# A fixed order on all engines for the first block of a fused attention and mixture-of-experts kernel, with two chunks multiplied undivided in place of eight

## The chip, the cores and the metric

The kernel runs on one core of a Trainium2 chip. A core has a matrix engine (TensorE, PE in the rows), VectorE (DVE), ScalarE (ACT) and GpSimd (POOL), each with a list of instructions of its own, and SyncE (SP), from whose queue this kernel's loads are issued. Engines wait for each other through semaphores. PEld is TensorE's loading of weights, which runs beside its products. The metric is the device time of one execution in microseconds (us).

## The reference

Attention of 2 batches, 8 heads, 768 queries and a head size of 64; its output feeds a dense two-layer network, and that one a routed network of 8 experts. Shortened:

```python
# attention: each query sees its own neighbours and one key and value per block of 32
k_sum = k.reshape(B, H, 24, 32, D).max(axis=3)
v_sum = v.reshape(B, H, 24, 32, D).mean(axis=3)
scores_l = where(abs(i - j) < 16, q @ k.T / 8, -1e9)
scores_s = q @ k_sum.T / 8 + log(32)
a = softmax(concat(scores_l, scores_s));  x = a @ concat(v, v_sum)     # 1536 x 512
# dense network, 512 -> 2048 -> 512
h = x @ w_in;  g = where(h > 0, h, exp(min(h, 0)) - 1);  x = g @ w_out
# routed network: for each token the expert e of the largest logit
e = argmax(x @ w_gate)
out = prob[e] * sigmoid(x @ w_output_gate)[e] * (relu(x @ w1[e]) @ w2[e])
```

## The kernel before

The 1536 tokens are 24 units of 64 queries, in four blocks j of 8, 4, 6 and 6 units (512, 256, 384, 384 tokens). The hidden layer of the dense network has 16 chunks c of 128. TensorE runs through all (j, c), with the attention of the next block between them: `mm_h(j,c)` forms h = x·w_in of a chunk, and two chunks later `mm_y(j,c)` adds g·w_out into one accumulator per 128 tokens.

Products keep float32 accuracy by division: an operand is split into a rounded high half and a low half, and a product is three, high·high, high·low and low·high. mm_h is 4×3 of these, mm_y one group of three per 128 tokens. "Undivided" means that mm_y multiplies the float32 operands themselves, one instruction per 128 tokens, which the trace shows as two records; the constant `C3` says for how many chunks of block 0.

What the other engines do for a chunk: ScalarE takes tanh and exp of h (`elu_act`, tiles elt and ele), VectorE forms elt and then elp, which is g (`elu_dve`). The second of these frees h's bank; there are two banks, so mm_h(j,c+2) waits for elp(j,c). For a divided chunk follow `split_g` (ScalarE gh, VectorE gl) and `split_w` (ScalarE the high half of wsp, VectorE the low one).

The weights come as 64-bit floats and are converted during block 0: per chunk and part (w_in "ri", w_out "ro") ScalarE's `conv_r` (two passes, or one for w_in chunks in `BITS`), VectorE's `conv_t` (one bit operation, or two for those in BITS) and `conv_f` (on POOL for the parts in `CP`), and for w_in the high and low halves, `conv_h` (ScalarE) and `conv_l` (VectorE). Raw w_out tiles and the wsp tiles share one pool of four buffers, the tiles of conversion, block keys ("kst") and value means ("vn1") one of five.

Orders: `START` is a list of steps by which all engines are ordered by hand, from the first maxima of keys to about the sixth chunk; `ORDER` is the order of the first loads. Behind START only TensorE's order is fixed (the loop over steps in the last function), and a scheduler places the other engines' and the queue's instructions. `PAIRS` gives the half step of a chunk at which a pair of units begins its attention, `SUM0` that of the block keys and value means of the second batch element.

Of the kernel before, what the change touches and what calls it, by code (L numbers as in the profile page):

```python
# [9 lines left out]
F32 = mybir.dt.float32  # L10
F32R = mybir.dt.float32r
# [72 lines left out]
class Prog:  # L84
# [86 lines left out]
    def conv_a(self, c, part):  # L171
        self.conv_r(c, part)
        self.conv_t(c, part)
        self.conv_f(c, part)

    def conv_b(self, c, part):
        if part == 0:
            self.conv_h(c)
            self.conv_l(c)

    def split_w(self, j, c):
        if j == 0 and c < C3:
            return
        nc = self.nc
        f = self.w[c, 1].bitcast(F32)
        w = self.ws.tile([128, 2, 512], F32R, tag="ws", name="wsp")
        nc.scalar.copy(w[:, 0], f)  # L187
        nc.vector.tensor_tensor(w[:, 1], f, w[:, 0].bitcast(F32), op=ALU.subtract)  # L188
        self.wsp[j, c] = w
# [273 lines left out]
    def x_lo(self, u):  # L463
        self.at5(u, 1)
# [19 lines left out]
    def elu(self, j, c):  # L484
        for i in range(2):
            self.elu_act(j, c, i)
        for i in range(2):
            self.elu_dve(j, c, i)

    def elu_act(self, j, c, i):  # L490
# [5 lines left out]
    def elu_dve(self, j, c, i):  # L496
# [112 lines left out]
    def part1(self):  # L609
# [10 lines left out]
        self.kT, self.cv, self.te, self.nmean = {}, {}, {}, 0  # L620
# [5 lines left out]
        pieces = [(c, p) for c in range(NF) for p in range(2)]  # L626
        wq, cq, dq = list(pieces), list(pieces), list(pieces)

        def wload(n):
            for x in wq[:n]:  # L630
                self.load_w(*x)
            del wq[:n]

        def conv(n=1):
            for _ in range(n):
                if dq and len(dq) > len(cq):
                    self.conv_b(*dq.pop(0))
                if cq and cq[0] in self.raw:
                    self.conv_a(*cq.pop(0))
# [19 lines left out]
        for j in range(1, NBLK):  # L659
            for n in range(UNITS[j]):  # L660
# [15 lines left out]
        at(14, self.route_consts)  # L676
        rank = {"at4": 0, "at3": 1, "at2": 2, "at1": 3, "at1bs": 4, "at5": 0}
        for p in range(NP):
            for hf in range(2):
                at(SUM0 + p - 2, self.load_sum, p, hf)  # L680
                at(SUM0 + p, self.red_sum, p, hf)
        for i in range(8):
            hs = SUM0 + 4 + 2 * i // 3
            at(hs - 2, self.load_v1, i)
            at(hs, self.mean_v1, i)
        at(SUM0 + 9, self.vsums2)
# [33 lines left out]
        with self.tc.manual_schedule(engines={mybir.EngineType.PE}):  # L720
            for i in range(len(steps)):
# [4 lines left out]
                wload(3)  # L726
                first = j == 0 and c in self.whole
                if j or c not in self.known:
                    self.mm_h(j, c, TB // 2 if j == 0 and c in self.half else 0)
                if not first:  # L730
                    conv()
# [6 lines left out]
                if i >= 2:
                    jj, cc = steps[i - 2]
                    if jj or cc not in self.summed:  # L740
                        self.mm_y(jj, cc)
                    if cc == NF - 1:
                        self.out_y(jj)
                if not first:
                    conv()
# [3 lines left out]
    def start_up(self):  # L749

        unit = dict(k=self.k_sum, s=self.scores, m=self.maxes, b=self.less_max, e=self.at1b, z=self.sums, r=self.recip, n=self.norm,
                    t=self.turn, c=self.turned, o=self.weighted, h=self.x_hi, l=self.x_lo, p=self.v_pad, x=self.max_k0, a=self.add_eps, M=self.mean_v0, K=self.keep_warm)
        part = dict(A=self.conv_r, B=self.conv_t, C=self.conv_f)
        self.split, self.half, self.whole, self.summed, self.known = (set() for _ in range(5))
        with self.tc.manual_schedule():
            for op in START.split():
                if op[0] == "H":
                    self.mm_h(0, int(op[1:]), 0, TB // 2)
                    self.half.add(int(op[1:]))
                    continue  # L760
                if op[0] in "GUVY":
                    c = int(op[1])
                    if op[0] == "G":
                        self.mm_h(0, c, TB // 2 if c in self.half else 0)
                        self.known.add(c)
                    elif op[0] == "Y":
                        self.mm_y(0, c)
                        self.summed.add(c)
                    else:
                        (self.elu_act if op[0] == "U" else self.elu_dve)(0, c, int(op[2]) - 1)  # L770
                        self.whole.add(c)
                    continue
                k, n = op[0], [int(i) for i in op[1:]]
                if k in unit:
                    unit[k](*n)
                elif k in part:
                    part[k](*n)
                    if k == "C" and n[1] == 1:
                        self.split.add((n[0], 1))
                elif k == "w":  # L780
                    self.window(*n)
                elif k == "P":
                    self.pad_v0()
                elif k == "D":
                    self.conv_h(*n)
                elif k == "E":
                    self.conv_l(*n)
                    self.split.add((n[0], 0))
# [811 lines left out]
```

## Time and profile before

| | |
|---|---|
| median of 3 runs | 533.13 us (532.93 to 533.65) |
| the profiled execution | 532.56 us, span 530.8 us |
| mean granted TensorE clock | 0.991 of full speed |
| TensorE busy | 515.1 us, 97% |
| VectorE busy | 332.1 us, 63% |
| ScalarE busy | 298.1 us, 56% |
| POOL busy | 55.9 us, 11% |

The times of the rows count from the start of the span. A row of a timeline gives start, duration, engine, line of the kernel, operation, output and inputs, and in brackets how long the engine was idle before and what ended that. Rows of equal instructions that follow each other are one row with a count, whose duration runs from the first start to the last end. Durations overlap a little: an instruction's last part runs beside the next one's first. [...] A wait for several semaphores is put down to the one that came last.

### The profile page before, as it was taken

What the parts mean: (1) busy time and instruction counts of PE and PEld (TensorE: products, weight loads), DVE (VectorE), ACT (ScalarE), POOL (GpSimd) and SP (SyncE); (2) the same over time, 40 slices, a digit from 0 to 9 for tenths busy, and PEclk for the clock granted to TensorE, in tenths of its full rate; (3) what the DMA queues carried; (4) which work ended last, traced back from release to release, by engine and by line L of the source; (5) the groups of instructions that cost most, each with busy time, mean ns of one, the idle gap of its engine ahead of it and who ended that gap; (6) DMA issues with size and microseconds to landing.
All of it is one profiled execution on the core that took longest, in us unless ns stands there. A gap on an engine that the chain in (4) does not pass through costs nothing. (4 is left out here: it accounts for less than half of the span.)

```text
span 530.8 us, 9764 instructions
## 1 busy us (share of the span) xinstructions
PE 515.1 (97%) x3299; PEld 404.9 (76%) x3299; DVE 332.1 (63%) x932; ACT 298.1 (56%) x704; POOL 55.9 (11%) x102
## 2 busy tenths in 40 slices
PE   8998999969999999999999999999999999999995
PEld 6485666758898888888999888888888566576884
DVE  4878999985687977785656799759421001545510
ACT  4798998834486767565546547443242232656521
POOL 2522000000000000000000000212511110100001
PEclk9999999979999999999999999999999999999999
DMA  8999834421022212100001006310498799494601
GB/s 288 404 404 314 278 123 143 147 71 31 27 103 81 75 36 91 57 25 16 0 2 61 1 25 233 101 61 1 122 354 279 299 340 348 157 364 137 220 23 43
DMA packets 37131, 78.08 MB, mean 147 GB/s; under 512 B 3951, under 2 KB 9807, under 8 KB 37072
## 3 DMA queue, kind: packets, MB, share of 16 engines
q1 hardware_dynamic: 34752, 70.02, 38.6%
q0 software_dynamic: 2320, 7.34, 3.9%
q8 instruction: 28, 0.46, 0.4%
q14 instruction: 31, 0.25, 0.2%
HBM read 100.37 MB, written 6.55 MB: 201 GB/s over the span
## 5 line engine op out<-in xcount | busy, mean ns | idle before, releaser
L481 PE MATMUL h<-xh,wi 128*128 128x384 f32 (+2 forms) x528 | 145.8, 344 | 6.5 <-DVE elp L506 6.5
L481 PEld LDWEIGHTS h<-xh,wi 128*128 128x128 f32 x528 | 95.0, 191 | 16.1 <-DVE elp L506 6.4
L536 PE MATMUL y<-wsp,gh 128*128 128x512 f32 x320 | 101.3, 398 | 0.0
L481 PE MATMUL h<-xl,wi 128*128 128x384 f32 (+2 forms) x264 | 88.2, 334 | 0.0
L536 PEld LDWEIGHTS y<-wsp,gh 128*128 128x128 f32 x320 | 57.7, 188 | 10.2 <-ACT ele L494 0.3
L536 PE MATMUL y<-wsp,gl 128*128 128x512 f32 x160 | 62.9, 393 | 0.0
L1255 DVE TENSOR_TENSOR holdl<-S,holdh 128x512 fp32r<-128x512 f32 x22 | 15.2, 690 | 72.5 <-ACT holdh L1251 53.7
L1223 PE MATMUL h<-w2s,holdh 128*128 128x512 f32 x176 | 59.9, 401 | 0.0
L1266 PE MATMUL y<-w2s,holdh 128*128 128x512 f32 x176 | 59.1, 398 | 0.0
L500 DVE SCALAR_TENSOR_TENSOR elt<-ele,elt 128x384 f32<-128x384 f32 (+2 forms) x64 | 36.4, 568 | 32.1 <-ACT ele L494 31.8
L481 PEld LDWEIGHTS h<-xl,wi 128*128 128x128 f32 x264 | 50.4, 191 | 5.0 <-issue 1.7
L494 ACT ACTIVATE elt<-h 128x384 f32<-128x384 f32 (+2 forms) x64 | 31.0, 484 | 32.5 <-PE h L481 31.6
L187 ACT CAST wsp<-wo 128x512 fp32r<-128x512 f32 x56 | 34.4, 617 | 21.7 <-PE y L536 21.7
L516 ACT CAST gh<-elp 128x384 fp32r<-128x384 f32 (+2 forms) x56 | 27.8, 496 | 31.0 <-DVE elp L506 21.7
L188 DVE TENSOR_TENSOR wsp<-wo,wsp 128x512 fp32r<-128x512 f32 x56 | 38.6, 689 | 8.7 <-ACT wsp L187 8.2
L1266 PEld LDWEIGHTS y<-w2s,holdh 128*128 128x128 f32 x176 | 33.1, 188 | 8.5 <-issue 1.6
L1223 PEld LDWEIGHTS h<-w2s,holdh 128*128 128x128 f32 x176 | 33.1, 188 | 8.1 <-ACT w2s L1291 0.8
L363 ACT ACTIVATE e<-e,nb 128x120 f32<-128x120 f32 x88 | 33.6, 384 | 10.0 <-DVE nb L350 10.0
L517 DVE TENSOR_TENSOR gl<-elp,gh 128x384 fp32r<-128x384 f32 (+2 forms) x56 | 30.0, 535 | 12.8 <-ACT gh L516 12.4
L1297 DVE TENSOR_TENSOR w2s<-wo,w2s 128x512 fp32r<-128x512 f32 x48 | 30.8, 686 | 8.8 <-ACT w2s L1291 7.3
L506 DVE SCALAR_TENSOR_TENSOR elp<-elt,h 128x384 f32<-128x384 f32 (+2 forms) x64 | 35.2, 550 | 1.2
L536 PEld LDWEIGHTS y<-wsp,gl 128*128 128x128 f32 x160 | 30.0, 188 | 6.9 <-DVE gl L517 0.3
(291 smaller groups left out, 845.8 us busy)
## 6 DMA issues: line engine op xcount, KB each, us to landing
wo<-in_w SPq DMA_DIRECT2D x9, 2048.0 KB
wo<-in_w SPq DMA_DIRECT2D x18, 1024.0 KB
ri<-in_w_in SPq DMA_DIRECT2D x16, 512.0 KB
ro<-in_w_out SPq DMA_DIRECT2D x16, 512.0 KB
wo<-in_w SPq DMA_DIRECT2D x32, 256.0 KB
w2p<-in_w SPq DMA_DIRECT2D x32, 256.0 KB
w2q<-in_w SPq DMA_DIRECT2D x24, 256.0 KB
k<-in_kw SPq DMA_DIRECT2D x18, 192.0 KB
```

The source lines that it names most:

```text
L187: nc.scalar.copy(w[:, 0], f)
L188: nc.vector.tensor_tensor(w[:, 1], f, w[:, 0].bitcast(F32), op=ALU.subtract)
L363: nc.scalar.activation(e[:, p], e[:, p], AF.Exp, bias=nb[:, p:p + 1], scale=-1.0, accum_out=sm[:, p:p + 1])
L481: nc.tensor.matmul(h, lhsT=w[:, wl, k * 128:k * 128 + 128], rhs=x[:, k, a:b], start=(n == 0), stop=(n == 11))
L494: self.nc.scalar.activation(self.te[j, c][i], self.h[j, c], AF.Exp if i else AF.Tanh, scale=1.0 if i else 0.5)
L500: nc.vector.scalar_tensor_tensor(t, e, 1.0, t, op0=ALU.add, op1=ALU.mult)
L506: nc.vector.scalar_tensor_tensor(p, t, 0.0, h, op0=ALU.min, op1=ALU.max)
L517: nc.vector.tensor_tensor(gl, p, gh.bitcast(F32), op=ALU.subtract)
L536: nc.tensor.matmul(self.y[j][t], lhsT=gx[:, sl], rhs=wx, start=(c == 0 and n == 0), stop=(c == NF - 1 and n == len(ops) - 1))
L1223: nc.tensor.matmul(self.h[s, hf], lhsT=x[:, k], rhs=w, start=(n == 0), stop=(n == 11))
L1266: nc.tensor.matmul(self.y2[s], lhsT=g[:, ks], rhs=w, start=(i == 0 and n == 0), stop=(i == 7 and n == 2))
L1297: (self.nc.gpsimd if eng == "Pool" else self.nc.vector).tensor_tensor(e[1], self.rw[i], e[0].bitcast(F32), op=ALU.subtract)
```

## The change

C3 falls from 8 to 2, so that mm_y of chunks 2 to 7 of block 0 is divided too, with split_w and split_g for them. BITS loses the w_in chunks 5, 10, 12 and 14. START is now the order of the whole of block 0 on all engines and of SyncE's loads (steps that begin with L), with the attention of units 8 to 11, the block keys and value means of the second batch element and the splits in single steps; ORDER and SUM0 are gone, and the loop begins at block 1. CP, WE, KE, NE, RADD and PADA, which say on which engine a conversion or a small step of a unit runs, have other entries. From mm_h(1,2) on TensorE's instructions are in the same order in both kernels.

```diff
-C3 = 8
+C3 = 2
-BITS = (0, 1, 2, 3, 5, 6, 8, 10, 12, 14)
-PAIRS = {8: 9, 10: 20, 12: 35, 14: 45, 16: 54, 18: 65, 20: 74, 22: 83}
+BITS = (0, 1, 2, 3, 6, 8)
+PAIRS = {12: 35, 14: 45, 16: 54, 18: 65, 20: 74, 22: 83}
-SUM0 = 26
-ORDER = "k3 k0 k2 k1 Q0 c0 Q1 c1 V4 V1 V2 W7 w1 V3 V0 Q2 W6 w1 w1 w1 w1 w1 w1 w1 w1 w1 w1 w1"
-NE = "PVVPPVPV"
-CP = ((1, 0), (1, 1))
-START = ...
+NE = "VVVPVVPV"
+CP = ((0, 0),)
+START = ...
     def split_w(self, j, c):
-        if j == 0 and c < C3:
-            return
...
+        self.w_high(j, c)
+        self.w_low(j, c)
...
-        for x in ORDER.split():
...
-        at(14, self.route_consts)
+        at(2 * NF, self.route_consts)
...
-            for i in range(len(steps)):
+            for i in range(NF, len(steps)):
...
     def start_up(self):
...
+        load = dict(k=self.load_k0, Q=self.load_q0, V=self.load_v0, W=self.load_kw, c=self.load_c, w=self.load_w, q=self.load_q, v=self.load_v, s=self.load_sum, u=self.load_v1)
+        part = dict(A=self.conv_r, B=self.conv_t, C=self.conv_f, D=self.conv_h, E=self.conv_l)
+        chunk = dict(U=self.elu_act, V=self.elu_dve, Y=self.mm_y, g=self.g_high, f=self.g_low, i=self.w_high, j=self.w_low)
...
         with self.tc.manual_schedule():
             for op in START.split():
...
```

In the rows of the order below the line numbers are each kernel's own. TensorE, mm_y(0,2) and what follows it (y: an accumulator of 128 tokens, wo: w_out as float32, elp: g, wsp, gh, gl: the halves; each undivided row is two records in the trace). Before:

```order
L536 MATMUL y_745<-wo_101,elp_770 128x512
L536 MATMUL y_746<-wo_101,elp_770 128x512
L536 MATMUL y_747<-wo_101,elp_770 128x512
L536 MATMUL y_748<-wo_101,elp_770 128x512
L481 MATMUL h_946<-xh0_217,wi5_875 128x512
L481 MATMUL h_946<-xl0_218,wi5_875 128x512
L481 MATMUL h_946<-xh0_217,wi5_875 128x512 x2
```

After:

```order
L543 MATMUL y_822<-wsp_788,gh_890 128x512 x2
L543 MATMUL y_822<-wsp_788,gl_899 128x512
L543 MATMUL y_823<-wsp_788,gh_890 128x512 x2
L543 MATMUL y_823<-wsp_788,gl_899 128x512
L543 MATMUL y_824<-wsp_788,gh_890 128x512 x2
L543 MATMUL y_824<-wsp_788,gl_899 128x512
L543 MATMUL y_825<-wsp_788,gh_890 128x512 x2
L543 MATMUL y_825<-wsp_788,gl_899 128x512
L482 MATMUL h_968<-xh0_165,wi5_893 128x512
```

Four undivided products became twelve divided ones, and mm_h(0,5) follows as it did.

VectorE between elt and elp of chunk 10 (vs: a value mean, wi15: low half of w_in of chunk 15, e: normalised weights of a unit, ks1: block keys, r2: the reciprocals of a pair). Before:

```order
L500 SCALAR_TENSOR_TENSOR elt_1300<-ele_1301,elt_1300 128x512
L249 TENSOR_REDUCE vs_1613<-vn1_1616 96x16
L169 SCALAR_TENSOR_TENSOR wi15_1566<-cv_t_1522,wi15_1566 128x512
L407 TENSOR_TENSOR e_1250<-e_1250,r2_1325 128x480
L407 TENSOR_TENSOR e_1256<-e_1256,r2_1325 128x480
L188 TENSOR_TENSOR wsp_1354<-wo_101,wsp_1354 128x512
L506 SCALAR_TENSOR_TENSOR elp_1305<-elt_1300,h_1271 128x512
```

After:

```order
L502 SCALAR_TENSOR_TENSOR elt_1393<-ele_1394,elt_1393 128x512
L524 TENSOR_TENSOR gl_1412<-elp_1318,gh_1367 128x512
L179 TENSOR_TENSOR wsp_1396<-wo_101,wsp_1396 128x512
L227 TENSOR_REDUCE ks1_97<-kst_1386 128x12
L167 SCALAR_TENSOR_TENSOR wi13_1329<-cv_t_1242,wi13_1329 128x512
L377 TENSOR_SCALAR r2_1417<-s2_1388 128x8
L378 RECIPROCAL r2_1417<-r2_1417 128x8
L508 SCALAR_TENSOR_TENSOR elp_1420<-elt_1393,h_1333 128x512
```

The value mean, the w_in half of chunk 15 and the normalisations stand elsewhere; in their place are a low half of g, block keys, the w_in half of chunk 13 and two short steps of a pair.

SyncE, the last raw w_out loads (ro) and what is queued around them (kst: keys for block keys, vn1: values for a mean, k, q and v2: a unit's). Before:

```order
L299 DMA k_1110<-in_kw 128x384
L301 DMA q_1109<-in_q 128x256
L124 DMA ro11_835<-in_w_out 128x1024
L124 DMA ro12_858<-in_w_out 128x1024
L124 DMA ro13_940<-in_w_out 128x1024
L124 DMA ro14_944<-in_w_out 128x1024
L124 DMA ro15_994<-in_w_out 128x1024
L232 DMA kst_1386<-in_kT 128x384
```

After:

```order
L122 DMA ro12_1438<-in_w_out 128x1024
L231 DMA vn1_1456<-in_vn1 96x512
L231 DMA vn1_1460<-in_vn1 96x512
L222 DMA kst_1491<-in_kT 128x384
L122 DMA ro13_1532<-in_w_out 128x1024
L294 DMA v2_100<-in_vw 96x512
L122 DMA ro15_1568<-in_w_out 128x1024
L222 DMA kst_1592<-in_kT 128x384
L122 DMA ro14_1601<-in_w_out 128x1024
L231 DMA vn1_1651<-in_vn1 96x512
```

The five loads that stood in a row are spread among loads of the block keys, value means and a unit's values, and ro15 stands ahead of ro14.

## Rows read from the trace of the kernel before

**Rows 1.** The page, the costliest group of instructions (busy, mean, idle before).

```profile
L481 PE MATMUL h<-xh,wi 128*128 128x384 f32 (+2 forms) x528 | 145.8, 344 | 6.5 <-DVE elp L506 6.5
```

**Rows 2.** Stretches: length, PE, PEld, DVE, ACT, POOL busy, clock, DMA share, GB/s.

```profile
40.00:50.00 10.00, 8.65 (x32) 5.75 (x31) 8.63 (x15) 8.89 (x15) 3.50 (x9) 1.00 1.05 310
100.00:110.00 10.00, 6.57 (x29) 5.10 (x28) 9.26 (x31) 7.39 (x24) 0.48 (x2) 0.93 0.58 177
110.00:120.00 10.00, 9.23 (x35) 7.56 (x36) 8.54 (x16) 4.52 (x9) 0.00 (x0) 0.73 0.02 6
130.00:140.00 10.00, 10.00 (x51) 8.54 (x50) 5.98 (x10) 4.17 (x9) 0.00 (x0) 1.00 0.00 0
```

**Rows 3.** Timeline of TensorE from 103 to 116 us.

```profile
103.69 0.62 PE L536 MATMUL y<-wsp,gh 128*128 128x512 f32 x2
...
106.18 0.39 PE L536 MATMUL y<-wsp,gl 128*128 128x512 f32 x1
110.77 0.80 PE L481 MATMUL h<-xh,wi 128*128 128x512 f32 x1 [4.20 <-DVE elp L506]
...
115.76 0.63 PE L536 MATMUL y<-wsp,gh 128*128 128x512 f32 x2
```

**Rows 4.** Timeline of VectorE in the same wait.

```profile
106.54 0.64 DVE L500 SCALAR_TENSOR_TENSOR elt<-ele,elt 128x512 f32<-128x512 f32 x1
107.10 0.68 DVE L249 TENSOR_REDUCE vs<-vn 96x16 f32<-96x512 f32 x1
107.70 0.68 DVE L169 SCALAR_TENSOR_TENSOR wi<-cv_t,wi 128x512 fp32r<-128x512 f32 x1
...
110.03 0.68 DVE L506 SCALAR_TENSOR_TENSOR elp<-elt,h 128x512 f32<-128x512 f32 x1
```

**Rows 5.** Timeline of TensorE: an undivided and a divided mm_y.

```profile
41.48 0.47 PE L481 MATMUL h<-xh,wi 128*128 128x512 f32 x1 [1.35 <-DVE elp L506]
...
44.32 3.59 PE L536 MATMUL y<-wo,elp 128*128 128x512 f32 x8
47.35 0.79 PE L481 MATMUL h<-xh,wi 128*128 128x512 f32 x1
47.99 0.40 PE L481 MATMUL h<-xl,wi 128*128 128x512 f32 x1
...
98.25 0.62 PE L536 MATMUL y<-wsp,gh 128*128 128x512 f32 x2
...
100.97 0.39 PE L481 MATMUL h<-xh,wi 128*128 128x512 f32 x1
```

**Rows 6.** Timeline of TensorE: scores of a pair, mm_y(0,15), mm_h(1,2).

```profile
142.71 0.31 PE L340 MATMUL S<-k,q 64*64 64x120 f32 x1
...
143.69 0.73 PE L536 MATMUL y<-wsp,gh 128*128 128x512 f32 x2
...
146.54 0.28 PE L481 MATMUL h<-xh,wi 128*128 128x256 f32 x1
```

**Rows 7.** Groups by shape, 0 to 147 us, ScalarE and VectorE.

```profile
L187 ACT CAST wsp<-wo 128x512 fp32r<-128x512 f32 x11 | 6.6, 614 | 5.7 <-PE y L536 5.7
...
L188 DVE TENSOR_TENSOR wsp<-wo,wsp 128x512 fp32r<-128x512 f32 x11 | 7.6, 687 | 2.4 <-ACT wsp L187 2.2
...
L149 DVE TENSOR_SCALAR cv_r<-ri 128x512 uint16<-128x512 uint16 x10 | 4.7, 473 | 0.0
```

**Rows 8.** Stretches again: start-up, elp(0,0) to gl(0,15), and 60 to 90.

```profile
10.00:41.30 31.30, 28.46 (x360) 18.84 (x360) 25.43 (x112) 24.98 (x79) 12.03 (x23) 1.00 1.03 404
41.30:139.07 97.77, 93.39 (x463) 65.80 (x464) 84.52 (x185) 72.70 (x149) 5.16 (x13) 0.97 0.47 144
60.00:90.00 30.00, 30.00 (x132) 18.90 (x131) 29.48 (x73) 29.91 (x63) 0.00 (x0) 1.00 0.54 172
```

**Rows 9.** Timelines of ScalarE and of SyncE: waits and issues of "ro".

```profile
53.90 0.79 ACT L132 ACTIVATE cv_r<-ro 128x512 uint16<-128x512 uint32 x1 [0.86 <-DMA ro<-in_w_out]
...
63.34 15.84 SPq L124 DMA_DIRECT2D ro<-in_w_out  x5
```

More of the change, by code (lines that the diff above doesn't have):

```diff
@@ L169, in conv_l, with w_high, w_low @@
         self.nc.vector.scalar_tensor_tensor(w[:, 1], f, 1.0 if c in BITS else 2.0, w[:, 0].bitcast(F32), op0=ALU.mult, op1=ALU.subtract)
[L171 to L179, printed above, removed]
-    def split_w(self, j, c):
-        if j == 0 and c < C3:
-            return
[L184 to L189, printed above, removed]
+    def split_w(self, j, c):
+        self.w_high(j, c)
+        self.w_low(j, c)
+    def w_high(self, j, c):
+        w = self.wsp[j, c] = self.ws.tile([128, 2, 512], F32R, tag="ws", name="wsp")
+        self.nc.scalar.copy(w[:, 0], self.w[c, 1].bitcast(F32))
+    def w_low(self, j, c):
+        w = self.wsp[j, c]
+        self.nc.vector.tensor_tensor(w[:, 1], self.w[c, 1].bitcast(F32), w[:, 0].bitcast(F32), op=ALU.subtract)
     def warm_up(self):
@@ L379, in at2, with recip2 @@
     def at2(self, u):
+        self.recip2(u)
+        for i in range(2):
+            self.norm(u + i)
+    def recip2(self, u):
         nc = self.nc
@@ L437, in weighted @@
     def weighted(self, u):
+        if u >= U0[1]:
+            first = self.u[u - u % 2]
+            if u % 2 == 0:
+                first["O"] = self.bank(self.psa, "S").rearrange("p (a q) -> p a q", a=NP)
+            self.product(u, first["O"][:, :, u % 2 * UQ:u % 2 * UQ + UQ])
+            return
         O = self.bank(self.psy, "y")[:, :NP * UQ].rearrange("p (a q) -> p a q", a=NP)
@@ L484, in elu, with elu_act @@
     def elu(self, j, c):
[L485 to L490, printed above, removed]
+        for f in self.elu_act, self.elu_dve:
+            for i in (1, 2):
+                f(j, c, i)
+    def elu_act(self, j, c, n):
+        i = n - 1
         if i == 0:
@@ L509, in split_g, with g_high, g_low @@
     def split_g(self, j, c):
-        nc = self.nc
-        if j == 0 and c < C3:
-            return
+        self.g_high(j, c)
+        self.g_low(j, c)
+    def g_high(self, j, c):
         p = self.g[j, c]
         gh = self.gp.tile([128, TB], F32R, tag="gh", name="gh")[:, :TBS[j]]
+        self.nc.scalar.copy(gh, p)
+        self.g[j, c] = p, gh
+    def g_low(self, j, c):
+        p, gh = self.g[j, c]
         gl = self.gp.tile([128, TB], F32R, tag="gl", name="gl")[:, :TBS[j]]
-        nc.scalar.copy(gh, p)
-        nc.vector.tensor_tensor(gl, p, gh.bitcast(F32), op=ALU.subtract)
-        self.g[j, c] = (gh, gl)
+        self.nc.vector.tensor_tensor(gl, p, gh.bitcast(F32), op=ALU.subtract)
+        self.g[j, c] = gh, gl
     def mm_y(self, j, c):
@@ L625, in part1 @@
         self.vt = [self.wo[:, 4 + u] if u < NS else self.v[u % self.NKV] for u in range(NU)]
[L626 to L639, printed above, removed]
         self.warm_up()
         self.consts()
-        for x in ORDER.split():
-            f = dict(Q=self.load_q0, V=self.load_v0, W=self.load_kw, w=wload, k=self.load_k0, c=self.load_c)[x[0]]
-            f(int(x[1:]))
         self.new_x(0)
@@ L648, in part1 @@
         self.start_up()
-        cq = [x for x in pieces if x not in self.w]
-        dq = [x for x in pieces if x not in self.split]
-        self.v_pad(U0[1])
         steps = [(j, c) for j in range(NBLK) for c in range(NF)]
@@ L657, in at @@
             todo.setdefault(hs, []).append((fn, args))
-        for j in range(1, NBLK):
+        for j in range(2, NBLK):
             for n in range(UNITS[j]):
@@ L675, in part1 @@
                 at(h0 + AT[3], self.at5, u)
-        at(14, self.route_consts)
+        at(2 * NF, self.route_consts)
         rank = {"at4": 0, "at3": 1, "at2": 2, "at1": 3, "at1bs": 4, "at5": 0}
[L678 to L686, printed above, removed]
+        at(2 * NF, self.vsums2)
         for j in range(NBLK - 1):
@@ L725, in part1 @@
                     self.new_x(j + 1)
[L726 to L731, printed above, removed]
+                self.mm_h(j, c)
                 self.split_w(j, c)
-                if i:
+                if i > NF:
                     self.split_g(*steps[i - 1])
-                if not first:
-                    self.elu(j, c)
+                self.elu(j, c)
@@ L737, in part1 @@
                 run(2 * i + 1)
[L738 to L745, printed above, removed]
+                jj, cc = steps[i - 2]
+                self.mm_y(jj, cc)
+                if cc == NF - 1:
+                    self.out_y(jj)
         assert not todo, todo
@@ L749, in start_up @@
     def start_up(self):
[L751 to L754, printed above, removed]
+        unit = dict(k=self.k_sum, s=self.scores, m=self.maxes, b=self.less_max, e=self.weights, z=self.sums, r=self.recip, R=self.recip2, n=self.norm, t=self.turn_of, c=self.turned,
+                    o=self.weighted, h=self.x_hi, l=self.x_lo, p=self.v_pad, x=self.max_k0, w=self.window, a=self.add_eps, M=self.mean_v0, P=self.pad_v0, K=self.red_sum, F=self.mean_v1, Z=self.keep_warm)
@@ L755, in start_up @@
+        load = dict(k=self.load_k0, Q=self.load_q0, V=self.load_v0, W=self.load_kw, c=self.load_c, w=self.load_w, q=self.load_q, v=self.load_v, s=self.load_sum, u=self.load_v1)
+        part = dict(A=self.conv_r, B=self.conv_t, C=self.conv_f, D=self.conv_h, E=self.conv_l)
+        chunk = dict(U=self.elu_act, V=self.elu_dve, Y=self.mm_y, g=self.g_high, f=self.g_low, i=self.w_high, j=self.w_low)
+        half = set()
+        for u in range(NV):
+            self.unit0(u)
         with self.tc.manual_schedule():
@@ L756, in start_up @@
             for op in START.split():
[L757 to L772, printed above, removed]
@@ L773, in start_up @@
-                k, n = op[0], [int(i) for i in op[1:]]
-                if k in unit:
-                    unit[k](*n)
+                k = op[0]
+                n = [int(i, 16) for i in op[2 if k == "L" else 1:]]
+                if k == "L":
+                    load[op[1]](*n)
                 elif k in part:
                     part[k](*n)
[L778 to L788, printed above, removed]
+                elif k == "H":
+                    self.mm_h(0, *n, 0, TB // 2)
+                    half.add(n[0])
+                elif k == "G":
+                    self.mm_h(0, *n, TB // 2 if n[0] in half else 0)
+                elif k in chunk:
+                    chunk[k](0, *n)
+                else:
+                    unit[k](*n)
@@ L791, in route_consts, with weights, turn_of @@
+    def weights(self, u):
+        if u < U0[1]:
+            self.at1b(u)
+            return
+        first = self.u[u - u % 2]
+        if "s2" not in first:
+            first["s2"] = self.sm.tile([128, 2, NP], F32, tag="s2", name="s2")
+        self.at1b(u, first["s2"][:, u % 2])
+    def turn_of(self, u):
+        self.turn(u, "T" if u < U0[1] else "ST"[u % 2])
     def route_consts(self):
```

27 lines of the change are left out of this document (14 added, 13 removed).

## The prediction, made before the changed kernel was run

> **What bounds the kernel now.** I read the page first: TensorE is busy 97% of the span, and the largest idle entry of any matmul group is 6.5 us in front of the x·w_in products, ended by VectorE's elp [rows 1]. So the time is TensorE's own work plus a few waits, and the next view is the table by stretches [rows 2]: behind the start-up TensorE lacks time in 40 to 50 and in 100 to 120 us; 130 to 140 reads 10.00, as do the others up to the milestone below. The change touches block 0 and what runs beside it, so I use one milestone: the first product of block 1's third chunk, mm_h(1,2), at 146.54 us [rows 6]. From there on TensorE's order is the same in both kernels and TensorE is nearly always busy, so what the change saves or costs at that point I pass to the end one for one.
>
> The wait at 110 us is the first place to understand. mm_y(0,9)'s last product starts at 106.18, and mm_h(0,12) should follow 0.23 us later at 106.41; it starts at 110.77, having waited for elp(0,10), which frees its bank: 4.36 us lost [rows 3]. On VectorE elt(0,10) was done at about 107.1, but a v mean, a low half of w_in, two normalisations and a split of w_out stood before elp(0,10) (110.03) [rows 4]: VectorE was not idle, it was doing work that was wanted later. The stall is paid twice. [...] The place costs 4.36+2.27 = 6.63 us.
>
> **The change, part by part.** *Six chunks divided.* An undivided mm_y is eight records, 44.32 to 47.35, and the next product, the second row after it, starts at 47.99 in place of 47.58: I take 47.99−0.23−44.32 = 3.44 us. A divided one, twelve products, takes 98.25 to 100.97 = 2.72 [rows 5]. Chunks 2 to 7 change, so TensorE loses 6×0.72 = 4.32 us. In return each needs four more instructions: on ScalarE a high half of w_out and one of g (0.62 each), on VectorE two low halves (0.69 each) [rows 7]; packed, VectorE starts the next one 0.60 us later (107.10 to 107.70 [rows 4]). That is 12×0.60 = 7.2 us for VectorE, and 12×0.53 ≈ 6.4 for ScalarE (same 0.09 of overlap).
>
> *Four chunks out of BITS.* For each, VectorE makes one bit operation in place of two; the second is 473 ns [rows 7], some 0.35 when packed as above: −1.4 us for VectorE. ScalarE gets a second pass each, at 0.79 [rows 9] unpacked 3.2; two of the four stand ahead of the stretch counted below.
>
> *The order of everything.* VectorE's list of after has 3.8 us more ahead of elp(0,0) (two last conversion steps 1.2, two normalisations 1.1, a low half 0.6, a bit step 0.3, two copies 0.5). From 10 us to the end of that elp at 41.3 VectorE was busy 25.43 of 31.30 us [rows 8], so there are 5.9 idle us to take it, but they are waits for loads and for TensorE, not free slots: I charge 0.5 us to the start of mm_h(0,2) (bounds 0, if all fits, and 1.5, if a quarter of the moved work and a load come late). It waits for just that elp now, 1.35 us idle, 41.48 [rows 5]. The scores of units 8 and 9 now stand ahead of mm_h(0,2), in that idle time: 0.98 us of TensorE's work leaves the stretch (the same 64 products took 142.71 to 143.69 [rows 6]).
>
> Behind elp(0,0) the order follows need. Up to elp(0,10), the one that caused the stall, VectorE's list has 56.0 us of work where it had 64.5 (7 conversion steps, 11 bit steps and 3 low halves fewer, 10 splits more), though what stands directly between elt(0,10) and elp(0,10) is still six instructions. TensorE reaches mm_h(0,12) about 59 us after mm_h(0,2) begins, if it never waits. So the 6.63 us should go. The work is not gone; it moves behind 110 us, where VectorE has free time: 5.98 of 10 us in 130 to 140 [rows 2].
>
> *TensorE alone.* mm_h(0,2) to the milestone: 146.54−41.48 = 105.06; minus 4.32, 6.63 and 0.98 gives 93.1 us.
>
> *The new waits.* The question is whether VectorE keeps up. From the end of elp(0,0) to the last split of g, gl(0,15), 41.30 to 139.07, it was busy 84.52 of 97.77 us, 86% [rows 8]. After, it has 84.5+7.2−1.4−3.8 = 86.5 us for it, and TensorE without waits leaves it 93.1−2.72+0.2 = 90.6. That is 95.5%, more than it reached over the whole stretch but less than in 60 to 90 us, where it was busy 29.48 of 30 with ScalarE at 29.91 and TensorE never waited [rows 8]. I take the mean of the two shares, 92.3%: 86.5/0.923 = 93.7, so TensorE waits 3.1 us in all, in small pieces. Bounds: 0 at 98%, 9.5 at 86% (86.5/0.864 = 100.1). ScalarE has 72.70+6.4+1.6 = 80.7 us in the same 90.6, less what was moved ahead, and is behind VectorE as a limit, though both are chained through tanh, exp, elt and elp. At three places (mm_y(0,3), mm_y(0,5), mm_y(0,8)) VectorE's summed list comes within 0.5 to 0.8 us of TensorE's, so small waits there are likely; the stall of rows 3 shows that a wait of 4 us brings the lower clock with it, while the 1.35 us at 41 us did not (granted 1.00 in 40 to 50) [rows 2, 5].
>
> *Loads.* SyncE's list now has the raw w_out loads spread between loads of block keys, v means and v. In before the last five were issued over 15.84 us from 63.34, at least 20 us before their use, waiting only for buffers [rows 9]. After, w_out splits of six more chunks share those four buffers, so the last six loads are issued when a buffer comes free, shortly before conversion. The trace has one such case: ScalarE waited 0.86 us at 53.90 [rows 9]. I count nothing for it beyond the waits above (VectorE's idle share in the mean contains it), from 0 to 6×0.86 = 5 us, some of it under slack. POOL loses one of its two conversion steps and some normalisations; nobody waits for it that is not counted.
>
> **Sum.** 41.48+0.5+93.1+3.1 = 138.2 in place of 146.54: 8.4 us. The profiled execution took 532.56 us (span 530.8), so 524.2; the median of the runs shown is 533.13, 0.57 more, and I give the forecast on that footing: **524.7 us**. With the kind bounds (no waits, no delay) it is 533.13−11.9 = 521.2; with 9.5 of waits and 1.5 of delay 532.2.
>
> [...] The rows show a ready instruction held by others in front of it: elp(0,10) could run at 107.2 and ran at 110.03 [rows 4]. [...]
>
> **Rivals.**
> A. *VectorE keeps its old share.* If the dependences between the engines, not the order, made up its 13 idle us, the same 86% gives waits of 9.5 us: 41.48+0.5+93.1+9.5 = 144.6, a gain of 2.0 us: 531.2 us. For: in 130 to 140 us VectorE is two fifths idle [rows 2], in waits for ScalarE. Against: that idle time is there because nothing was left to do.
> B. *Slower: late w_out loads hold ScalarE and VectorE.* The last six raw tiles are loaded into buffers that earlier splits must release; those are released by TensorE's mm_y, TensorE waits for the elp behind the waiting conversion, and the loop runs at the pace of buffer release plus load. Two stalls like that of rows 3 with their slow clock, 2×6.63 = 13.3 us in place of 3.1, would give 41.48+0.5+93.1+13.3 = 148.4: 535.0 us. It decides from 11.4 us of waits (about 1.9 per load of the six); measured is 0.86 for one [rows 9]. For: the splits add six users of four buffers. Against: the DMA share was 0.54 in 60 to 90 us [rows 8], so a transfer finds room.
> C. *The order does not do what it says:* the stall is only moved to another chunk, and only the 4.32 and 0.98 us come. 533.13−5.3+0.5 = 528.3 us. For: six instructions still stand between elt(0,10) and elp(0,10). Against: VectorE's list reaches that point 8.5 us earlier.
>
> **Chances.** Forecast, waits under 5 us (521 to 526.5): 0.54. C, one stall like the old one left (526.5 to 530): 0.19. A (530 to 533): 0.13. B (above 533): 0.14. The range that leaves out two in ten runs from 520.8, below the kind bound by the spread of the runs, to 531.8, above A. The measurement can tell about 0.2%, 1.07 us, from no change: faster means under 532.06, slower over 534.20. Of A three parts in five and everything left of it are faster: 0.54+0.19+0.07 = 0.80; same 0.07; slower 0.13.
>
> **What would show it.** In the profile of the changed kernel: the milestone mm_h(1,2) near 138; mm_y of chunks 2 to 7 twelve records of 2.72 us; no 4 us gap before mm_h(0,12), and a granted clock of 1.00 in 100 to 120 us; VectorE near 9.2 of 10 us in every stretch up to 130, in place of a full first half and a half empty second. A milestone at 144 with many waits for elp or gl says A; ScalarE or VectorE waiting for "ro" in the list of waits, for 2 us each, says B; one gap with a clock of 0.7 to 0.8 behind it says C. My sum is wrong at its root if mm_h(0,2) starts later than 43, or if time appears or goes behind the milestone.

## The result: faster by 1.1%, and the profile after

The changed kernel took 527.7 us (median of 4 runs, 526.98 to 528.11) against 533.03 for the kernel before beside it: a ratio of 0.9891 (95% interval 0.9876 to 0.9907), 5.3 us. The forecast was 524.7, 8.4 less than before; the time lies in the range, the gain is under two thirds of the forecast. The profiled execution took 526.98 us with a span of 525.2. Three sets of runs below hold one execution far above the others (572.53, 640.39 and 2899.98 us): the medians contain it, the ratios leave it out.

The first table is the one by stretches, columns as in [rows 2]; "(x…)" counts instructions, and the clock is a share of full speed.

```profile
40.00:50.00 10.00, 9.47 (x62) 6.47 (x63) 9.76 (x32) 9.69 (x18) 0.53 (x2) 1.00 1.06 316
50.00:60.00 10.00, 10.00 (x38) 6.95 (x37) 10.00 (x21) 10.00 (x25) 0.00 (x0) 1.00 0.53 193
80.00:90.00 10.00, 10.00 (x59) 7.97 (x58) 9.84 (x18) 9.43 (x18) 0.00 (x0) 1.00 0.32 97
100.00:110.00 10.00, 10.00 (x45) 8.27 (x45) 10.00 (x20) 9.54 (x18) 0.00 (x0) 1.00 0.39 131
110.00:120.00 10.00, 10.00 (x47) 8.27 (x46) 10.00 (x19) 9.03 (x17) 0.34 (x1) 1.00 0.58 185
120.00:130.00 10.00, 7.51 (x61) 5.84 (x61) 8.27 (x15) 4.10 (x8) 0.99 (x2) 0.96 0.15 44
130.00:140.00 10.00, 10.00 (x76) 8.56 (x75) 6.12 (x26) 4.25 (x16) 0.82 (x2) 0.87 0.13 37
```

TensorE's column reads 10.00 in every stretch from 50 to 120 us: the stall of [rows 3] is gone, and the six divided chunks brought no wait in its place, with VectorE at 9.1 to 10.0. What is missing lies in 120 to 130 (7.51), and 130 to 140 shows a granted clock of 0.87. The timeline of TensorE there:

```profile
121.17 0.60 PE L412 MATMUL T<-c,e 128*120 128x128 f32 x4
121.70 0.69 PE L449 MATMUL S<-et,v 120*64 120x64 f32 x16
122.31 0.74 PE L543 MATMUL y<-wsp,gh 128*128 128x512 f32 x2
122.90 0.40 PE L543 MATMUL y<-wsp,gl 128*128 128x512 f32 x1
...
125.30 0.69 PE L449 MATMUL S<-et,v 120*64 120x64 f32 x16
126.86 0.38 PE L482 MATMUL h<-xh,wi 128*128 128x256 f32 x1 [0.87 <-ACT xh L455]
128.85 0.39 PE L482 MATMUL h<-xl,wi 128*128 128x256 f32 x1 [1.61 <-DVE xl L462]
...
131.08 1.05 PE L543 MATMUL y<-wsp,gh 128*128 128x512 f32 x2
...
134.56 0.28 PE L482 MATMUL h<-xh,wi 128*128 128x256 f32 x1
...
139.91 0.28 PE L482 MATMUL h<-xh,wi 128*128 128x256 f32 x1
```

After mm_y(0,13) (122.31) TensorE does the weighted product of unit 11 (125.30; unit 10's is at 121.70) and wants to start block 1 with mm_h(1,0). Its operand x is the pair's product, copied by ScalarE (xh) and subtracted by VectorE (xl). It waits 0.87 us for xh and 1.61 for xl, and then runs slowly: the eleven products of mm_h(1,0) that are left at 128.85 take until 131.08 = 2.23 us where the same eleven of mm_h(1,2) take 1.32, and mm_y(0,14) takes 3.48 in place of 2.72. The low clock so costs some 1.7 us beside the waits. The milestone of the prediction, mm_h(1,2), begins at 139.91; before it was 146.54 [rows 6]. VectorE and ScalarE in those microseconds:

```profile
126.31 0.68 DVE L179 TENSOR_TENSOR wsp<-wo,wsp 128x512 fp32r<-128x512 f32 x1
126.91 0.68 DVE L524 TENSOR_TENSOR gl<-elp,gh 128x512 fp32r<-128x512 f32 x1
127.52 0.68 DVE L179 TENSOR_TENSOR wsp<-wo,wsp 128x512 fp32r<-128x512 f32 x1
128.12 0.68 DVE L462 TENSOR_TENSOR xl<-S,xh 128x512 fp32r<-128x512 f32 x1
```
```profile
125.18 0.62 ACT L518 CAST gh<-elp 128x512 fp32r<-128x512 f32 x1 [0.61 <-PE y L543]
125.71 0.61 ACT L175 CAST wsp<-wo 128x512 fp32r<-128x512 f32 x1
126.23 0.58 ACT L455 CAST xh<-S 128x512 fp32r<-128x512 f32 x1
```

xh is ready at 126.8, and xl starts at 128.12: two low halves of w_out and one of g, for mm_y of chunks 14 and 15, stand before it. Nobody is slow here; the three steps from the product to x stand late in three lists.

### The profile page after: what moved, and what is told of

Read it like the earlier page. It is cut to its first block, busy times and chain, and to the rows that moved or that the text cites. A ratio compares the mean times of both kernels' runs of the same rounds, so it can differ in the third digit from the quotient of the medians.

```text
span 525.2 us, 9833 instructions
## 1 busy us (share of the span) xinstructions
PE 511.6 (97%) x3325; PEld 409.6 (78%) x3325; DVE 337.1 (64%) x945; ACT 305.1 (58%) x715; POOL 54.4 (10%) x102
## 5 line engine op out<-in xcount | busy, mean ns | idle before, releaser
L482 PE MATMUL h<-xh,wi 128*128 128x384 f32 (+2 forms) x528 | 142.8, 338 | 2.5 <-DVE elp L508 1.5
L543 PE MATMUL y<-wsp,gh 128*128 128x512 f32 x368 | 117.3, 400 | 0.0
L543 PEld LDWEIGHTS y<-wsp,gh 128*128 128x128 f32 x368 | 66.8, 190 | 12.3 <-issue 0.5
L543 PE MATMUL y<-wsp,gl 128*128 128x512 f32 x184 | 72.5, 394 | 0.0
L175 ACT CAST wsp<-wo 128x512 fp32r<-128x512 f32 x62 | 38.0, 617 | 16.8 <-PE y L543 16.0
L179 DVE TENSOR_TENSOR wsp<-wo,wsp 128x512 fp32r<-128x512 f32 x62 | 42.6, 689 | 6.3 <-ACT wsp L175 6.0
L518 ACT CAST gh<-elp 128x384 fp32r<-128x384 f32 (+2 forms) x62 | 31.5, 508 | 23.5 <-DVE elp L508 12.8
L524 DVE TENSOR_TENSOR gl<-elp,gh 128x384 fp32r<-128x384 f32 (+2 forms) x62 | 34.0, 549 | 12.2 <-ACT gh L518 11.9
L543 PEld LDWEIGHTS y<-wsp,gl 128*128 128x128 f32 x184 | 34.7, 188 | 8.0 <-DVE gl L524 0.3
```

The costliest lines, as they stand in the source:

```text
L175: self.nc.scalar.copy(w[:, 0], self.w[c, 1].bitcast(F32))
L179: self.nc.vector.tensor_tensor(w[:, 1], self.w[c, 1].bitcast(F32), w[:, 0].bitcast(F32), op=ALU.subtract)
L482: nc.tensor.matmul(h, lhsT=w[:, wl, k * 128:k * 128 + 128], rhs=x[:, k, a:b], start=(n == 0), stop=(n == 11))
L518: self.nc.scalar.copy(gh, p)
L524: self.nc.vector.tensor_tensor(gl, p, gh.bitcast(F32), op=ALU.subtract)
L543: nc.tensor.matmul(self.y[j][t], lhsT=gx[:, sl], rhs=wx, start=(c == 0 and n == 0), stop=(c == NF - 1 and n == len(ops) - 1))
```

## The experiments

Theory T: the other engines keep pace with TensorE up to the border of the blocks, and the changed kernel loses time only there, by where the end of block 1's attention stands in the lists. Rival R: VectorE and ScalarE are full, and x is late for that reason. All medians stand against runs of the kernel before on the same chip. "From 2 to M" is the time from mm_h(0,2) to mm_h(1,2) in the profile (before 105.06, changed 98.43). The first four kernels ran on one chip, the next four on a second and the last three on a third; e1_tail and e1_again, the same kernel on two of them, differ by 0.45 us in the median and by 0.17 from 2 to M.

| kernel | median us | before beside it | ratio (95%) | from 2 to M |
|---|---|---|---|---|
| e1_tail | 523.13 | 533.61 | 0.9808 (0.9749 to 0.9866) | 94.09 |
| e2_c8 | 530.67 | 533.61 | 0.9937 (0.9912 to 0.9963) | 101.73 |
| e3_tail_c8 | 528.18 | 533.61 | 0.9889 (0.9858 to 0.9920) | 98.39 |
| e4_before_c2 | 539.43 | 533.61 | 1.0110 (1.0084 to 1.0136) | 109.96 |
| e1b_la | 525.99 | 533.72 | 0.9856 (0.9830 to 0.9883) | 95.44 |
| e5_dve12 | 529.45 | 533.72 | 0.9929 (0.9911 to 0.9947) | 100.45 |
| e6_c1 | 525.10 | 533.72 | 0.9841 (0.9823 to 0.9858) | 95.24 |
| e7_bits | 524.10 | 533.72 | 0.9820 (0.9802 to 0.9838) | 94.82 |
| after_again | 527.24 | 534.24 | 0.9886 (0.9853 to 0.9919) | 97.98 |
| e1_again | 523.58 | 534.24 | 0.9813 (0.9784 to 0.9842) | 94.26 |
| e9_c1_pool | 525.35 | 534.24 | 0.9854 (0.9820 to 0.9888) | 96.30 |

**The end of the attention earlier (e1_tail).** In START, t is the transposition of weights, c its copy, o the product, h and l are xh and xl; behind these letters a and b are units 10 and 11. Y is mm_y, U and V are elu_act and elu_dve, i and j the high and low half of w_out, g and f those of g; behind these a to f are chunks 10 to 15:

```diff
-Ue1 nb Yc tb ca Ue2 ... Uf1 Uf2 oa cb ge F3 Be1 Vf1 Yd Ce1 ie ob Vf2 fe je jf gf ha F4 ff la
+Ue1 nb tb ca oa Yc Ue2 ... Uf1 Uf2 cb ob ha ge F3 Be1 Vf1 Yd Ce1 ie Vf2 la fe je jf gf F4 ff
```

> The changed kernel with the end of the attention of units 10 and 11 moved ahead: transposition, weighted product, xh and xl no longer queued behind mm_y(0,12), mm_y(0,13) and the last splits. Theory T (the changed kernel loses time only at the border of the blocks, because of where these steps stand): no wait before mm_h(1,0), no low clock behind it, mm_h(1,2) at about 135.5 in place of 139.91, time 527.7 - 4.4 = 523.3 us (522.7 to 524.0). Rival R (VectorE and ScalarE are full, so the steps only push the splits of chunks 14 and 15 back): TensorE waits before mm_y(0,14) or mm_y(0,15) instead, mm_h(1,2) at 138 to 140, 526 to 528 us.

Its stretch from mm_h(0,2) to the end of mm_h(1,0) (columns as in [rows 2]), and TensorE at the border and at the milestone:

```profile
41.35:127.30 85.95, 85.89 (x452) 67.28 (x453) 83.81 (x184) 78.16 (x160) 3.25 (x2) 1.00 0.52 166
```
```profile
125.97 0.28 PE L482 MATMUL h<-xh,wi 128*128 128x256 f32 x1
126.08 0.28 PE L482 MATMUL h<-xl,wi 128*128 128x256 f32 x1
...
135.50 0.28 PE L482 MATMUL h<-xh,wi 128*128 128x256 f32 x1
```

TensorE was busy 85.89 of 85.95 us, xl is read 0.11 us after xh, and the milestone is at 135.50 as T said. R falls as the cause of the wait: VectorE, busy 83.81 us (97.5%), did everything in time. The same kernel beside the changed one on one chip (e1_again, after_again) was 3.7 us faster by the medians, and its stretch from 2 to M 3.72 shorter:

> The first experiment's kernel again: T expects 4.3 us less than the run beside it, 523.3, mm_h(1,2) 94.1 us after mm_h(0,2); if the first session's difference was the chip's, less than 3 us.

> The changed kernel as it is, for a comparison on one chip with the next run: 527.7 (527.0 to 528.1), 5.3 us below the kernel before, mm_h(1,2) 98.4 us after mm_h(0,2).

Both medians came out as said, the difference 0.6 us below the 4.3 of T; why stands under the hardware below. e1_tail is faster than the kernel before and than the changed one.

**Only xh and xl earlier (e1b_la).** The product stays behind mm_y(0,13).

```diff
-Yd Ce1 ie ob Vf2 fe je jf gf ha F4 ff la
+Yd Ce1 ie ob Vf2 ha la fe je jf gf F4 ff
```

> The changed kernel with xh and xl of units 10 and 11 taken out of the queue of the last splits, but the transposition and the product left where they are (behind mm_y(0,12) and mm_y(0,13)). T: the 1.61 us in which TensorE waits for xl shrink to the one step xh to xl, about 0.6, the 0.87 for xh stay, since that product is still the last thing TensorE does before mm_h(1,0); mm_h(1,2) at 138.5 to 139, 526.5 us (526.0 to 527.2). If the queue on VectorE were the whole cause: all 4.4 us back, 523.3.

```profile
126.81 0.38 PE L482 MATMUL h<-xh,wi 128*128 128x256 f32 x1 [0.69 <-ACT xh L455]
127.55 0.38 PE L482 MATMUL h<-xl,wi 128*128 128x256 f32 x1 [0.35 <-DVE xl L462]
...
137.06 0.28 PE L482 MATMUL h<-xh,wi 128*128 128x256 f32 x1
```

The wait for xl is 0.35 us, the one for xh 0.69. The milestone came at 137.06, earlier than the 138.5 expected: the lower clock did not follow these shorter waits (granted 1.00 from 127.3 to 140 us), and that part had not been counted; the time, 525.99, lies at the lower end of what T said. So by single profiles, of the 4.3 us at the border 3.0 come from the lists of ScalarE and VectorE, with the clock that followed, and 1.3 from the product's place on TensorE.

**The order without the division (e2_c8, e3_tail_c8).** C3 = 8 again, the steps i, j, g and f of chunks 2 to 7 taken out of START; the second also with the edit of e1_tail. The other entries of the change (BITS, CP and the rest) stay.

```diff
-C3 = 2
+C3 = 8
```

> The changed kernel with chunks 2 to 7 undivided as before (C3 = 8, the 24 splits taken out of the order, nothing else). T: TensorE needs 6 x 0.72 = 4.3 us more, arrives at the border 4.3 us later, finds x there and waits for nothing; mm_h(1,2) at 139.5 to 140, time 527.7 (527.1 to 528.2): the division gains nothing in this order. If the division's saving does come through to the end, as the prediction's sum has it: 527.7 + 4.3 = 532.0.

> Both edits: attention's end ahead and chunks 2 to 7 undivided. T: nothing waited at the border in the second run, so nothing is won by the earlier end: the time of the second run within 0.5, 527.2 to 528.2, and 4.3 us more than the first run. R: the first run gains nothing, and this one is as slow as TensorE's own work makes it, also 527.5, no more than 1.5 above the first.

```profile
130.99 0.38 PE L482 MATMUL h<-xh,wi 128*128 128x256 f32 x1 [0.87 <-ACT xh L455]
132.02 0.39 PE L482 MATMUL h<-xl,wi 128*128 128x256 f32 x1 [0.65 <-DVE xl L462]
...
143.09 0.28 PE L482 MATMUL h<-xh,wi 128*128 128x256 f32 x1
...
130.00:140.00 10.00, 8.48 (x68) 7.33 (x68) 4.92 (x11) 3.15 (x8) 0.00 (x0) 0.83 0.10 25
```

The rows show TensorE of e2_c8 at the border, the milestone, and the stretch from 130 to 140 us; the profile is that of the slowest of its ten executions (532.36). T missed e2_c8: it took 530.7 (529.07 to 532.36), between the 527.7 of T and the 532.0 of the sum. It had been thought that a TensorE that comes 4.3 us later finds x there. But x hangs on TensorE's own product, the last instruction before mm_h(1,0), so the wait came with it at the slower pace too: again 0.87 us for xh, and 0.65 for xl, with a granted clock of 0.83 in 130 to 140. Without that wait (e3_tail_c8) the undivided kernel needs 98.39 us and the divided one (e1_tail) 94.09: the division is worth 4.30, as the sum had it (4.32). The difference of the two medians is about 5 us. e3_tail_c8 lies within T's 527.2 to 528.2, but not for T's reason: it is 2.5 us faster than e2_c8, where T expected the same. In the changed kernel itself, with its wait at the border, the division is worth less: 101.73−98.43 = 3.30, and 3.0 by the medians. Order and entries without the division gave 2.9 us by the medians of e2_c8.

**The division without the order (e4_before_c2).**

```diff
-C3 = 8
+C3 = 2
```

> The kernel before with C3 = 2 alone: the division without the fixed order. If the stall at 110 us stays as it is (4.4 + 2.3 us), the time falls by 4.3: 528.7. T (VectorE was full from 60 to 84 us and its order was not by need): the 7.2 us of new splits come ahead of elp(0,10), the stall grows by 7.2 + 4.3 less what idle time takes up, and the gain is gone: 531 to 538.

TensorE's waits, in the list of waits, and the stretch from 60 to 70 us (the granted clock is the third number from the end):

```profile
PE h L481 <- DVE elp L506: 4.6, 2, 3.2
PE y L536 <- ACT wsp L187: 4.3, 1, 4.3
PE y L536 <- DVE wsp L188: 3.0, 2, 2.1
...
60.00:70.00 10.00, 5.85 (x13) 4.29 (x14) 9.95 (x34) 10.00 (x29) 0.00 (x0) 0.51 0.40 129
```

It is 5.8 us slower than before. The scheduler put the new splits of w_out behind other conversions, TensorE waited 11.9 us in five places, and the granted clock of 60 to 70 us, where two of them end, is 0.51. The expected 531 to 538 was a little low. The same division gains 4.3 us in an order made for it and costs 5.8 in the old one.

**How full VectorE is (e5_dve12, e6_c1, e7_bits).** All on e1_tail. The first forms twelve low halves twice, the second divides chunk 1 too, the third has the ten entries of BITS of before.

```diff
-j2 ... jd
+j2 j2 ... jd jd
```
```diff
-C3 = 2
+C3 = 1
-V12 kb C40 G2 U21 Y0 Lw70
+V12 kb C40 G2 i1 g1 U21 j1 f1 Y0 Lw70
```
```diff
-BITS = (0, 1, 2, 3, 6, 8)
+BITS = (0, 1, 2, 3, 5, 6, 8, 10, 12, 14)
```

> The first experiment's kernel with the low half of w_out formed twice for chunks 2 to 13: 12 x 0.60 = 7.2 us more on VectorE and nothing else. In that experiment VectorE was busy 83.81 of the 85.95 us up to mm_h(1,1), 97.5%, and TensorE waited for nothing. If VectorE is at its limit there: 7.2 less the 2.1 idle, TensorE waits some 5 us, 528 us (526.5 to 530, more if the low clock joins). If its busy time holds work done ahead that only fills gaps: within 1.5 us of the first experiment, 523 to 524.5.

> The first experiment's kernel with chunk 1 divided as well (C3 = 1, its four splits put right behind its elp). TensorE needs 0.72 us less, VectorE gets 1.2 more in 40 to 60 us, where it was busy 19.76 of 20. If VectorE is at its limit: no gain, 523.1 to 524.5. If not: 522.4.

> The first experiment's kernel with the ten entries of BITS as before: VectorE 4 bit operations more (1.4 us), ScalarE 4 passes fewer (2.6). If VectorE is at its limit and ScalarE is not: 0.5 to 1.5 us slower, 523.6 to 524.6. If the two engines are bound through each other's results, or there is room: 523.1 within 0.4.

```profile
PE h L482 <- DVE wi L167: 1.8, 2, 1.0
PE h L482 <- DVE elp L508: 0.8, 2, 0.5
PE y L543 <- DVE gl L524: 0.7, 2, 0.5
```
```profile
59.80 0.47 PE L482 MATMUL h<-xh,wi 128*128 128x512 f32 x1 [0.55 <-DVE elp L508]
...
63.59 0.50 PE L543 MATMUL y<-wsp,gl 128*128 128x512 f32 x1 [0.34 <-DVE gl L524]
```

The first rows are TensorE's waits in e5_dve12, the last two its timeline in e6_c1. VectorE is at its limit in e1_tail. In e5_dve12 7.2 us more of its work cost 100.45−94.09 = 6.4 us on the path, in waits of up to 1.0 us for halves of weights, elp and gl; VectorE was busy 91.06 of the 92.30 us from 41.8 to 134.1, 98.7%. With chunk 1 divided (e6_c1) TensorE has 0.72 us less to do and took 1.15 more, all of it lost by 74 us; the time, 525.1, is above the 524.5 that was expected at most. e7_bits decides nothing. From 2 to M it took 0.7 us more, 0.56 of them in mm_h of chunks 12 and 13, with a low half of w_in and an elp late; but in the changed kernel that place cost nothing in the first profile and a wait of 0.82 in after_again, and e7_bits' executions (523.24 to 525.37) overlap with those of e1_tail (522.83 to 524.82). So two chunks undivided is about as far as the division goes in this order.

**Work from VectorE to POOL (e9_c1_pool).** e6_c1 with three last conversion steps on POOL:

```diff
-CP = ((0, 0),)
+CP = ((0, 0), (4, 0), (5, 0), (3, 1))
```

> Chunk 1 divided, and the last conversion step of (4, w_in), (5, w_in) and (3, w_out) on POOL, which is idle there: VectorE gets 1.8 us less in the stretch where the divided chunk 1 gave it 1.2 more. If VectorE was what kept that run from its gain: TensorE's waits behind 59 us go, mm_h(1,2) 93.4 to 94.1 us after mm_h(0,2), 522.4 to 523.3. If POOL's longer step (1.3 us for 0.6) or something else holds the chain: no better than chunk 1 divided alone, 95.2 and 525.

Timelines of POOL (GpSimd) and of VectorE:

```profile
51.22 1.62 POOL L156 TENSOR_TENSOR cv_t<-cv_t,cv_r 128x512 int32<-128x512 int32 x1 [4.01 <-DMA ri<-in_w_in]
55.75 1.61 POOL L156 TENSOR_TENSOR wo<-cv_t,cv_r 128x512 int32<-128x512 int32 x1 [2.92 <-DVE cv_t L149]
```
```profile
48.19 0.68 DVE L524 TENSOR_TENSOR gl<-elp,gh 128x512 fp32r<-128x512 f32 x1
...
51.60 1.79 DVE L167 SCALAR_TENSOR_TENSOR wi<-cv_t,wi 128x512 fp32r<-128x512 f32 x1
...
56.12 1.78 DVE L524 TENSOR_TENSOR gl<-elp,gh 128x512 fp32r<-128x512 f32 x1
...
59.43 0.68 DVE L167 SCALAR_TENSOR_TENSOR wi<-cv_t,wi 128x512 fp32r<-128x512 f32 x1
```

No gain; from 2 to M 96.30, worse than the 95.24 of e6_c1. The third POOL step (45.92 to 47.21) ran beside an elp, which took its usual 0.68 us, and into a wait of VectorE. But while POOL runs the other two (51.22 to 52.84, 55.75 to 57.36), VectorE's instruction takes 1.79 and 1.78 us in place of 0.68: POOL takes 0.6 us of work off VectorE and holds it up for 1.1. Alone the same two instructions took 0.68 us each (the first and the last VectorE row). Why these two were held up and the elp was not, no run shows.

## Why the direction was right and the size too large, step by step

The sum said 41.48+0.5+93.1+3.1 = 138.2 for the milestone; it was 41.48+0+94.1+4.3 = 139.9.

- *Start of mm_h(0,2), +0.5:* none. It began at 41.48 in both profiles; what was moved ahead of elp(0,0) found room in VectorE's idle time (busy 28.28 us from 10.00 to 41.30, before 25.43). In the other profiles with the new order it began at 40.89 to 42.16, so the term is within what executions and entries make.
- *TensorE alone, 93.1:* 94.09 in e1_tail, where it waits for nothing. The division's 4.32 was right (4.30), and the old stall with its 6.63 us was gone as said. Of those, 4.36 were the wait and 2.27 slow products: in the kernel before mm_h(0,12) took 110.77 to 115.76 = 4.99 us, and the twelve products from 100.97 to 103.69 take 2.72 [rows 3, 5]; the granted clock reads 0.50 from 109 to 115 us. The term was 1.0 too small: units 8 to 11 now go one by one, 0.61 us for a unit's product (121.70 to 122.31) where a pair took 1.08, and the two wide products behind it take 0.59 us in place of 0.45. Added up by kind from the two timelines, 0.29 of the 1.0 are the units' products (2.46 in place of 2.17), 0.16 the scores of units 10 and 11 (1.14 in place of 0.98), and the rest, some 0.5, lies in mm_h and mm_y, which now follow such small products more often; that this is why was not tested. The pair's product in the kernel before, and the mm_y behind it:

```profile
83.53 1.15 PE L449 MATMUL S<-et,v 120*64 120x64 f32 x32
84.61 1.55 PE L536 MATMUL y<-wo,elp 128*128 128x512 f32 x3
```

- *New waits, 3.1:* 4.3, waits and low clock together, and for another reason. The step that failed is the one from VectorE's busy share (92.3%) to TensorE's waits (3.1 us, in small pieces). VectorE reached 97.5% without TensorE waiting once (e1_tail), near the upper of the two shares (98) and far above the mean that was taken (92.3); the old order's share was no measure for an order made by need. What came in its place was one wait that the sum did not look for, 0.87+1.61 us at the border with the clock of 0.87 behind it, since it followed elp and gl and never asked when block 1's x would be ready. The bounds (0 to 9.5) held it; that 4.3 lies near 3.1 is luck.
- *Loads, rival B:* fell. ScalarE waited 2.5 us for "ro" and VectorE 0.9 up to 126 us in the changed kernel, and TensorE waited for none of it.
- *Rival C* (528.3) gave the best number: one wait with the low clock behind it, in another place than before. But it rested on the six instructions between elt and elp of chunk 10, and there nothing waited; that its number was the nearest is luck.
- *Rival A* fell with VectorE's 97.5%. Its mechanism is the one that shows when more work is added (e5_dve12, e6_c1).
- *One for one behind the milestone:* not quite. The gain is 6.63 us at the milestone, 6.52 170 us later, 6.03 at the last product and 5.58 in the profiled time. A product of block 3 and the last product, before and after:

```profile
316.16 0.33 PE L481 MATMUL h<-xh,wi 128*128 128x384 f32 x1
...
524.17 0.39 PE L1266 MATMUL y<-w2s,holdh 128*128 128x512 f32 x1
```
```profile
309.64 0.33 PE L482 MATMUL h<-xh,wi 128*128 128x384 f32 x1
...
518.14 0.39 PE L1233 MATMUL y<-w2s,holdh 128*128 128x512 f32 x1
```

So the dense network keeps the gain, and about 1 us goes in the routed part and in the output behind it. e1_tail, 11.04 us ahead at the milestone and 9.45 in its profiled time, lost 1.6 there. It is not chance: from the milestone to the end of the profiled time the old order needs 386.0 and 386.1 us (before, e4_before_c2), seven profiles of the new one 386.7 to 387.6, and its other four 388.3 to 389.7 (the last section returns to these). The cause of the first difference stays open.

- *A ready instruction behind others* [rows 4] *came again, at the border:* xl, free to run at 126.8, ran at 128.12 behind two that began after that (126.91 and 127.52).

Together, against the profiled time: 1.2 us of waits, 1.0 of TensorE's own and 1.05 behind the milestone, less the 0.5 that didn't come, are 2.75; measured 526.98−524.2 = 2.8.

## What to carry to other kernels

VectorE at 97.5% of its time made nobody wait with its list in the order of need (e1_tail), and at 83% (8.27 of 10 us in 120 to 130 of the changed kernel) it made TensorE wait 1.61 us where the list wasn't: judge a fixed order by following each operand of the first instruction behind a border back through the lists, not by busy shares. Moving work off the bound engine paid only where the engine that took it had its list in order: the same edit was worth 4.3 us less or 5.8 us more. When a stall goes, look what the same engine reads next that was never late before.

## What the runs showed of the hardware

The lower clock does not follow each wait of the same size. The changed kernel waited 0.87 and 1.61 us in the first profile, and a granted clock of 0.87 followed in 130 to 140 us; in after_again it waited 0.87 and 1.52, and that stretch reads 1.00:

```profile
128.30 0.38 PE L482 MATMUL h<-xh,wi 128*128 128x256 f32 x1 [0.87 <-ACT xh L455]
130.20 0.39 PE L482 MATMUL h<-xl,wi 128*128 128x256 f32 x1 [1.52 <-DVE xl L462]
...
130.00:140.00 10.00, 9.80 (x82) 8.52 (x83) 6.17 (x27) 4.45 (x16) 0.82 (x2) 1.00 0.18 45
```

There the border cost about 1.3 us less, part of it given back by a wait of 0.82 at 103 us for a low half of w_in. What the border costs is therefore some 3 to 4.3 us, by the execution. Shorter waits were followed by the lower clock too (0.87 and 0.65 us by 0.83 in e2_c8), and others not (0.69 and 0.35 in e1b_la, with 1.00 behind them), so what the prediction read from its rows, 4 us bring it and 1.35 do not, is not the whole of it.

The clock also falls at a second place, in some executions. Between 340 and 360 us a stretch of 10 us reads 0.83 to 0.90 in the profiles of e2_c8, e1b_la, e6_c1 and e7_bits and 1.00 in the nine others, with TensorE busy 10.00 in all of them; a wait of 0.6 to 0.7 us at 324 to 339 us stands in all thirteen. Those are the four that need 0.7 us or more longer from the milestone to the end than all others; the mean clock of the profiled execution is 0.994 or 0.995 in e1b_la, e6_c1 and e7_bits and 0.992 in e2_c8 (its border among it), against 0.997 or 0.998 in the others with the new order but the changed kernel's first (0.993, its border among it). In e2_c8 two equal products from 355.07 us take 0.85 us to the next one, and two from 357.83 take 0.46. The medians contain this, and the column from 2 to M does not.

And of the three POOL steps that ran beside an instruction of VectorE in e9_c1_pool, two lengthened it from 0.68 us to 1.79 and 1.78, by 1.1 each, more than the 0.6 that a step takes over; beside the third an elp took 0.68.
